# Splitting 64-bit weights on a Trainium2 core: from the square and six mask operations to a scaled copy, a sign and five operations

## The chip, the cores and the metric

The kernel runs on one core of one Trainium2 chip. The metric is the device time of one execution in microseconds. Three executions of the kernel before took 776.67, 776.81 and 775.69 us; the median is 776.67 us.

## What is computed

All inputs are stored as 64-bit floating-point numbers. Three stages follow one another: attention in which a query sees only the keys of its own cluster, a feed-forward layer with a quadratic gate, and a gated layer behind a normalisation.

```python
q_assign = np.argmax(np.einsum('bhsd,hcd->bhsc', q_n, c_n), axis=-1)   # 2 x 8 heads, 768 tokens, 64 wide, 16 clusters
k_assign = np.argmax(np.einsum('bhsd,hcd->bhsc', k_n, c_n), axis=-1)
mask = q_assign[:, :, :, None] == k_assign[:, :, None, :]
attn = softmax(where(mask, scale * q @ k.T, -1e9)) @ v
...
h = x @ w_in                                    # x: 1536 x 512, w_in: 512 x 2048
g = np.where(h >= 1, h, np.where(h <= -1, 0.0, (h + 1) ** 2 / 4))
x = g @ w_out                                   # 2048 x 512
...
xn = x / np.sqrt(np.mean(x * x, axis=-1, keepdims=True) + 1e-06) * rms_g
g, val = xn @ w_gate, xn @ w_val                # 512 x 1536 each
out = (g / (1.0 + np.exp(-g)) * val) @ w_out2   # 1536 x 512
```

## The kernel before

**Products of two halves.** TensorE multiplies numbers that are rounded to a short form. Each factor x is held as a high part, x rounded to that form, and a low part, the rest; a product takes three matmuls, high by high, high by low and low by high. Activations are rounded by ScalarE (a cast) and the rest is taken by VectorE or POOL (a subtraction).

**Weights.** The weights come as 92 slices of 128 x 512 numbers, in the order of the list `stream`. 68 of them are loaded: SP issues two transfers for each (`w_load`, L512), which bring the high 32-bit words (`raw`), and the words one 16-bit step further on (`mid`). `conv_ops` (L546) turns them into the high part `w[:, 0]` and the low part `w[:, 1]`: one square of ScalarE (L565, or L572 while `pace["on"]` is false, in the attention's last part) and six operations of VectorE (L566, L568, L570, L576, L578, L580). The square is large where the number is large enough to matter, and L576 uses it to drop the smallest numbers. L566, L570 and L578 are one-input mask operations; L568 (mask and or), L576 and L580 take two inputs.

**Sums of gate weights.** The other 24 slices are not loaded. They are sums and differences of halves of the gate and value weights, which let the gated layer do with seven products (`term_unit`) in place of eight. `w_sums` (L526) queues six additions for each pair of weights; POOL makes them (L534), one behind each operation of a conversion. A slice of such a sum is converted by one cast of ScalarE (L557) and one subtraction of VectorE (L559). In the order printed below the sums are `s_0` and `s_1`.

**The order of the work.** The program writes all engines' instructions in one order. `units()` is the list of the steps of TensorE (each 0.6 to 2.8 us long by the planner's own numbers); `unit()` issues one and adds its time to `pace["pe"]`. `drain()` issues what the steps before need next on the other engines. Then `fill()` (L1011) issues conversion operations as long as the time that the planner has counted for VectorE, `pace["dve"]`, with the cost of the next one stays below `pace["pe"]`. Each engine works off its own instructions in the order in which they were issued.

**The two places that matter here.** (1) Behind the first layer, `turn_pair` (L728) transposes two tiles of Y and forms three combinations of them: ScalarE copies v (L751) and casts (L752, L753), VectorE subtracts (L756 to L758), ScalarE casts the four results (L762) and POOL takes the rests (L764). It does so four times; ahead of each the tiles Y are completed by an addition of VectorE (L802) and squared by ScalarE for the normalisation (L830). (2) In the gated layer each group of 128 columns is computed by seven terms. Term 1 goes into a bank of accumulators B, term 5 into E, term 2 into A. ScalarE copies B to u before term 6 adds to it, E to e before term 3 does, B to v before term 7 does, and B to w before term 4 does (all L713). TensorE has to wait for each of these copies before it may go on in that bank. ScalarE's silu (L672), the cast of a finished gate (L668) and, for the third block of tokens, the casts of transposed tiles (L863) lie in between.

Of the kernel before, what the change touches and what calls it, by code (L numbers as in the profile page):

```python
# [28 lines left out]
GROUPS2 = [3, 3, 3, 3]  # L29
NPLACES = 24  # L30
LOCK = 0.3
HB = 6
NP = B * H // 2
HALF = S // 2
# [6 lines left out]
def clustered_attention_two_ffn(  # L41
# [464 lines left out]


    W = {}
    stream = []
    cv = {"loaded": 0, "at": 0, "ops": [], "left": 0, "limit": 6, "soon": NPLACES - 6}  # L510

    def w_load():  # L512
        n = cv["loaded"]
        cv["loaded"] += 1
        layer, i, m = stream[n]
        if m < 0:
            return
        rows = slice(128 * m, 128 * m + 128)
        src = (w_in[m], w_out[rows])[i] if layer == 1 else (w_gate[m], w_val[m], w_out2[rows])[i]
        raw, mid, t = fp["raw"](n)  # L520
        nc.sync.dma_start(raw.rearrange("p n w -> p (n w)"), src.bitcast(U32))

        nc.sync.dma_start(mid.rearrange("p n w -> p (n w)").bitcast(U16)[:, 0:2047], src.bitcast(U16)[:, 1:2048])
        cv[n] = (raw[:, :, 1], mid[:, :, 0], t, raw[:, :, 0].bitcast(F32))
# [4 lines left out]
    def w_sums(i, m, w, f):  # L529
# [8 lines left out]
        if i == 0:  # L538
            fp["f"] = f
            return  # L540
        f1, f2 = fp.pop("f"), f
        s, r = (pf.tile([128, 512], F32, tag="s", bufs=3, name=f"s{m}_{n}") for n in range(2))
        op(s[:, left], f2[:, left], f2[:, right], ALU.add)
# [5 lines left out]
    def conv_ops(n):  # L549
# [11 lines left out]
        hi, mid, t, sq = cv.pop(n)  # L561
        tf = t.bitcast(F32)

        if pace["on"]:
            nc.scalar.activation(sq, hi.bitcast(F32), AF.Square, scale=2.0 ** 15)  # L565
        nc.vector.tensor_scalar(t, hi, 3, 0x3FFFF000, op0=ALU.logical_shift_left, op1=ALU.bitwise_and)  # L566
        yield
        nc.vector.scalar_tensor_tensor(t, hi, 0xC0000000, t, op0=ALU.bitwise_and, op1=ALU.bitwise_or)  # L568
        yield
        nc.vector.tensor_scalar(mid, mid, 0x01FFFFFF, None, op0=ALU.bitwise_and)  # L570
        if not pace["on"]:
            cv["square"] = lambda: nc.scalar.activation(sq, hi.bitcast(F32), AF.Square, scale=2.0 ** 15)  # L572
        yield
        square()

        nc.vector.scalar_tensor_tensor(w[:, 0], sq, 1.125 * 1.125, tf, op0=ALU.is_ge, op1=ALU.mult)  # L576
        yield
        nc.vector.tensor_scalar(t, w[:, 0].bitcast(U32), 0xFF800000, None, op0=ALU.bitwise_and)  # L578
        yield
# [5 lines left out]
    def conv(n_ops=1):  # L585

        for _ in range(n_ops):
            if not cv["ops"]:
                if cv["at"] >= cv["limit"] or not room():
                    return False  # L590
                while cv["loaded"] <= cv["at"]:
                    w_load()
                cv["ops"] = [conv_ops(cv["at"])]
                cv["left"] = 6 if stream[cv["at"]][2] >= 0 else 2
                cv["at"] += 1
            pace["dve"] += cost()
            next(cv["ops"][0])
            tick()
            cv["left"] -= 1
            if fp["gp"]:  # L600
                fp["gp"].pop(0)()
            if not cv["left"]:
                cv["ops"] = []
            while cv["loaded"] < cv["limit"] and not any(m >= 0 for _, _, m in stream[cv["at"]:cv["loaded"]]):
                w_load()
# [399 lines left out]
    pace = {"on": False, "pe": 0.0, "dve": 0.0, "post": 0.0}  # L1005

    def cost():
        m, n = (stream[cv["at"] - 1][2], cv["left"]) if cv["ops"] else (stream[cv["at"]][2], 6) if cv["at"] < len(stream) else (0, 0)
        return (0.6 if n == 1 else 0.0) if m < 0 else (0.6 if n % 2 else 0.335) + LOCK * bool(fp["gp"])

    def fill():  # L1011

        while pace["on"] and pace["dve"] + cost() <= pace["pe"] + SLACK[layer_of()]:
            if not conv(1):
                break

# [320 lines left out]
```

## Time and profile before

| | |
|---|---|
| median of three runs | 776.67 us (775.69 to 776.81) |
| the profiled execution | 775.95 us, span 774.2 us |
| TensorE busy | 768.3 us, 99% of the span |
| VectorE busy | 609.9 us, 79% |
| ScalarE busy | 391.9 us, 51% |
| POOL busy | 288.9 us, 37% |
| chain that ended last | PE 92%, DVE 2%, ACT 2%, DMA 1%, POOL 1% |

In the rows, PE is TensorE, DVE VectorE, ACT ScalarE and SP the engine that issues the transfers. A row of a timeline gives the start and the duration of an instruction, and in brackets how long its engine sat idle before it and what ended that. The times of matmuls overlap: what a matmul takes in a row of matmuls is read from one start to the next, not from its duration. The span is the time from the first to the last instruction, and the execution's own time is 1.75 us longer.

### The profile page before, as it was taken

The numbers are of one execution on the slowest core, as the hardware profiler recorded it, in microseconds if no ns is written. First come the engines' busy times: TensorE is split into PE (matmuls) and PEld (weight loads), VectorE is DVE, ScalarE is ACT, GpSimd is POOL, SyncE is SP. The second block draws the span as 40 slices with busy tenths as digits, with TensorE's granted clock in tenths as the row PEclk, the third lists the DMA queues.
The fourth block names the chain that finished last, engine by engine and source line by source line (L and its number), as shares of the span: only waits on it lengthen the run. The fifth ranks groups of instructions, "written<-read, shape, count | busy, mean of one in ns | idle before, by whom it ended". The sixth has DMA issues, their size and how long they took to land.

```text
span 774.2 us, 10868 instructions
## 1 busy us (share of the span) xinstructions
PE 768.3 (99%) x3714; PEld 592.0 (76%) x3714; DVE 609.9 (79%) x1106; ACT 391.9 (51%) x758; POOL 288.9 (37%) x313
## 2 busy tenths in 40 slices
PE   8999999999999999999999999999999999999998
PEld 4666666776558888888888888878888888888887
DVE  6776887776578999877668768899999799988743
ACT  7676767665567655444334447544545315423430
POOL 5878999998000000000001206441454334423400
PEclk9999999999999999999999999999999999999999
DMA  7657665573144676444334310125563343434013
GB/s 202 173 138 182 156 150 131 150 172 113 55 142 143 218 237 218 170 137 163 109 109 136 99 37 0 32 95 181 187 213 109 104 160 128 154 109 163 1 41 123
DMA packets 32679, 103.41 MB, mean 134 GB/s; under 512 B 5016, under 2 KB 5356, under 8 KB 32624
## 3 DMA queue, kind: packets, MB, share of 16 engines
q1 hardware_dynamic: 32612, 102.72, 43.8%
q8 instruction: 29, 0.48, 0.3%
q14 instruction: 26, 0.21, 0.1%
q10 hardware_dynamic: 12, 0.00, 0.0%
HBM read 81.02 MB, written 3.15 MB: 109 GB/s over the span
## 4 chain that ended last, share of the span: by engine, by line
PE 92%; DVE 2%; ACT 2%; DMA 1%; POOL 1%; issue 1%; ACTq 0%; DVEq 0%; POOLq 0%
PE h L624 25%; PE y L788 9%; PE y L787 9%; PE y L786 9%; PE pv L406 8%; PE B L651 8%; PE mp L336 5%; PE sc L385 4%; PE sc L386 4%; PE E L651 4%; PE A L651 2%; PE sum L425 1%; DMA kraw<-kT 1%; PE simt L171 1%; PE sum L414 1%
## 5 line engine op out<-in xcount | busy, mean ns | idle before, releaser
L338 DVE TENSOR_REDUCE M<-mp 128x1 f32<-128x384 f32 x186 | 94.6, 552 | 44.6 <-PE mp L336 44.4
L534 POOL TENSOR_TENSOR bits<-place 128x256 f32<-128x256 f32 x18 | 17.6, 1000 | 265.5 <-DVE place L580 265.5
L398 POOL TENSOR_TENSOR acc<-acc,P 128x384 f32<-128x384 f32 x112 | 109.2, 1004 | 4.1 <-ACT P L388 3.5
L388 ACT ACTIVATE P<-sc 128x384 f32<-128x384 f32 x192 | 82.3, 490 | 42.1 <-PE sc L386 34.1
L624 PE MATMUL h<-xh,aa 128*128 128x512 f32 x280 | 89.3, 390 | 0.1
L802 DVE TENSOR_TENSOR Y<-y,Y 128x512 f32<-128x512 f32 (+1 forms) x85 | 57.8, 681 | 39.6 <-PE y L788 39.3
L639 ACT ACTIVATE a<-h,half_b 128x512 f32<-128x512 f32 x48 | 33.0, 687 | 81.4 <-PE h L624 80.4
L406 PE MATMUL pv<-P,v 128*64 128x384 f32 x384 | 70.6, 492 | 0.0
L385 PE MATMUL sc<-aa,bb 112*128 112x384 f32 x192 | 66.1, 344 | 0.0
L386 PE MATMUL sc<-aa,bb 97*128 97x384 f32 x192 | 65.0, 338 | 0.0
L624 PE MATMUL h<-xh,bb 128*128 128x512 f32 x200 | 64.2, 389 | 0.0
L624 PEld LDWEIGHTS h<-xh,aa 128*128 128x128 f32 x280 | 52.5, 188 | 12.9 <-DVE a L641 0.8
L565 ACT ACTIVATE raw<-raw 128x512 f32<-128x512 f32 x62 | 42.2, 680 | 38.1 <-DMA raw<-w_out 12.4
L641 DVE SCALAR_TENSOR_TENSOR a<-h,a 128x512 f32<-128x512 f32 x48 | 33.1, 690 | 29.7 <-ACT a L640 29.7
L624 PE MATMUL h<-xl,aa 128*128 128x512 f32 x140 | 54.5, 389 | 0.0
L568 DVE SCALAR_TENSOR_TENSOR bits<-raw,bits 128x512 uint32<-128x512 uint32 x68 | 51.7, 760 | 1.6
L336 PE MATMUL mp<-bb,aa 112*128 112x384 f32 x186 | 52.5, 360 | 0.3
L406 PEld LDWEIGHTS pv<-P,v 128*64 128x64 f32 x384 | 25.4, 136 | 31.4 <-issue 30.3
L336 PEld LDWEIGHTS mp<-bb,aa 112*128 112x128 f32 x186 | 32.2, 189 | 15.3 <-issue 5.5
L624 PEld LDWEIGHTS h<-xh,bb 128*128 128x128 f32 x200 | 37.5, 188 | 7.8
L719 POOL TENSOR_TENSOR w<-w,e 128x512 f32<-128x512 f32 x12 | 16.8, 1396 | 60.9 <-ACT w L713 60.9
L624 PE MATMUL h<-xl,bb 128*128 128x512 f32 x100 | 38.9, 389 | 0.0
(307 smaller groups left out, 1987.3 us busy)
## 6 DMA issues: line engine op xcount, KB each, us to landing
raw<-w_out SPq DMA_DIRECT2D x28, 512.0 KB
mid<-w_out SPq DMA_DIRECT2D x28, 511.8 KB
raw<-w_in SPq DMA_DIRECT2D x16, 512.0 KB
mid<-w_in SPq DMA_DIRECT2D x16, 511.8 KB
raw<-w_gate SPq DMA_DIRECT2D x12, 512.0 KB
raw<-w_val SPq DMA_DIRECT2D x12, 512.0 KB
mid<-w_gate SPq DMA_DIRECT2D x12, 511.8 KB
mid<-w_val SPq DMA_DIRECT2D x12, 511.8 KB
```

The lines of the kernel that those rows point to most:

```text
L336: nc.tensor.matmul(mp, A[0:112, h, 0, 128 * qt:128 * qt + 128], Bk[0:112, h, 0, HALF * n:HALF * n + HALF], start=True, stop=True)
L338: nc.vector.tensor_reduce(st["M2", p][:, j, n:n + 1], mp, axis=AX.X, op=ALU.max)
L385: nc.tensor.matmul(sc, Bk[0:112, h, 0, ks], A[0:112, h, 0, qs], start=True, stop=False)
L386: nc.tensor.matmul(sc, Bk[0:97, h, 1, ks], A[0:97, h, 1, qs], start=False, stop=True)
L388: nc.scalar.activation(P, sc, AF.Exp, scale=0.125)
L398: nc.gpsimd.tensor_tensor(acc, acc, P, op=ALU.add)
L406: nc.tensor.matmul(pv[64 * h:64 * h + 64, 0:HALF], st["v", p][:, h, kt], st["P", p, i, h], start=(kt == 0), stop=(kt == NT - 1))
L624: nc.tensor.matmul(h, w[:, wi, fs], x[:, kc, cs], start=(n == 0), stop=(n == 11))
L651: nc.tensor.matmul(h, w[:, wi, fs], x[xi][:, kc], start=start and n == 0, stop=(n == 5), skip_group_check=not start)
L786: nc.tensor.matmul(y[:, c], g[:, 0, fs], w[:, 0, c], start=(m == m0), stop=False)
L787: nc.tensor.matmul(y[:, c], g[:, 0, fs], w[:, 1, c], start=False, stop=False)
L788: nc.tensor.matmul(y[:, c], g[:, 1, fs], w[:, 0, c], start=False, stop=(m == ms[-1]))
```

## The change

The square and the first two operations of VectorE are replaced. ScalarE now makes a copy of the high words, scaled by 2^-112 (new L571), and then the sign of the high words in their own place (new L572). VectorE shifts and masks the scaled copy (new L580), and the high part is that, times the sign (new L582). The scaling drops the smallest numbers by itself. So a slice takes two operations of ScalarE and five of VectorE. The planner's costs follow (`cost()`, five operations). Besides, `fill()` no longer begins a slice while `landed` of that slice is later than `pace["pe"]`: for a loaded slice `landed` is the planner's estimate of the landing (4.2 per load, one behind the other, and 1.0), and for a sum 8.0 behind the time at which its additions were queued. Behind the first inserted lines the numbers of the changed kernel are higher: L557 becomes L563, L559 L565, L713 L719, L764 L770, L802 L808.

```diff
--- before.py
+++ after.py
@@ -29,6 +29,7 @@
 GROUPS2 = [3, 3, 3, 3]
 NPLACES = 24
 LOCK = 0.3
+LOAD, LAND, SUMS = 4.2, 1.0, 8.0
 HB = 6
 NP = B * H // 2
 HALF = S // 2
@@ -506,6 +507,7 @@
 
 
     W = {}
+    landed = {}
     stream = []
     cv = {"loaded": 0, "at": 0, "ops": [], "left": 0, "limit": 6, "soon": NPLACES - 6}
 
@@ -515,6 +517,8 @@
         layer, i, m = stream[n]
         if m < 0:
             return
+        cv["free"] = max(cv.get("free", 0.0), pace["pe"]) + LOAD
+        landed[n] = cv["free"] + LAND
         rows = slice(128 * m, 128 * m + 128)
         src = (w_in[m], w_out[rows])[i] if layer == 1 else (w_gate[m], w_val[m], w_out2[rows])[i]
         raw, mid, t = fp["raw"](n)
@@ -538,6 +542,8 @@
         if i == 0:
             fp["f"] = f
             return
+        for k in range(2):
+            landed[stream.index((2, k, -m - 1))] = pace["pe"] + SUMS
         f1, f2 = fp.pop("f"), f
         s, r = (pf.tile([128, 512], F32, tag="s", bufs=3, name=f"s{m}_{n}") for n in range(2))
         op(s[:, left], f2[:, left], f2[:, right], ALU.add)
@@ -561,19 +567,19 @@
         hi, mid, t, sq = cv.pop(n)
         tf = t.bitcast(F32)
 
+        def sides():
+            nc.scalar.activation(sq, hi.bitcast(F32), AF.Copy, scale=2.0 ** -112)
+            nc.scalar.activation(hi.bitcast(F32), hi.bitcast(F32), AF.Sign)
+
+        cv["square"] = sides
         if pace["on"]:
-            nc.scalar.activation(sq, hi.bitcast(F32), AF.Square, scale=2.0 ** 15)
-        nc.vector.tensor_scalar(t, hi, 3, 0x3FFFF000, op0=ALU.logical_shift_left, op1=ALU.bitwise_and)
-        yield
-        nc.vector.scalar_tensor_tensor(t, hi, 0xC0000000, t, op0=ALU.bitwise_and, op1=ALU.bitwise_or)
-        yield
+            square()
         nc.vector.tensor_scalar(mid, mid, 0x01FFFFFF, None, op0=ALU.bitwise_and)
-        if not pace["on"]:
-            cv["square"] = lambda: nc.scalar.activation(sq, hi.bitcast(F32), AF.Square, scale=2.0 ** 15)
         yield
         square()
-
-        nc.vector.scalar_tensor_tensor(w[:, 0], sq, 1.125 * 1.125, tf, op0=ALU.is_ge, op1=ALU.mult)
+        nc.vector.tensor_scalar(t, sq.bitcast(U32), 3, 0x7FFFF000, op0=ALU.logical_shift_left, op1=ALU.bitwise_and)
+        yield
+        nc.vector.tensor_tensor(w[:, 0], tf, hi.bitcast(F32), op=ALU.mult)
         yield
         nc.vector.tensor_scalar(t, w[:, 0].bitcast(U32), 0xFF800000, None, op0=ALU.bitwise_and)
         yield
@@ -591,7 +597,7 @@
                 while cv["loaded"] <= cv["at"]:
                     w_load()
                 cv["ops"] = [conv_ops(cv["at"])]
-                cv["left"] = 6 if stream[cv["at"]][2] >= 0 else 2
+                cv["left"] = 5 if stream[cv["at"]][2] >= 0 else 2
                 cv["at"] += 1
             pace["dve"] += cost()
             next(cv["ops"][0])
@@ -1005,12 +1011,14 @@
     pace = {"on": False, "pe": 0.0, "dve": 0.0, "post": 0.0}
 
     def cost():
-        m, n = (stream[cv["at"] - 1][2], cv["left"]) if cv["ops"] else (stream[cv["at"]][2], 6) if cv["at"] < len(stream) else (0, 0)
-        return (0.6 if n == 1 else 0.0) if m < 0 else (0.6 if n % 2 else 0.335) + LOCK * bool(fp["gp"])
+        m, n = (stream[cv["at"] - 1][2], cv["left"]) if cv["ops"] else (stream[cv["at"]][2], 5) if cv["at"] < len(stream) else (0, 0)
+        return (0.6 if n == 1 else 0.0) if m < 0 else (0.6 if n in (1, 3) else 0.335) + LOCK * bool(fp["gp"])
 
     def fill():
 
         while pace["on"] and pace["dve"] + cost() <= pace["pe"] + SLACK[layer_of()]:
+            if not cv["ops"] and landed.get(cv["at"], 0.0) > pace["pe"]:
+                break
             if not conv(1):
                 break
```

TensorE's and SP's instructions keep their order. On the other three engines the change moves instructions. The first place is ScalarE at the beginning of the gated layer. In the rows below, u, e, v and w are the copies out of the banks, `s_0` and `s_1` the sums of gate weights that are cast, and a the silu. Before:

```order
L713 COPY u_5190<-B_5183 128x512
L713 COPY e_5211<-E_5204 128x512
L672 ACTIVATE a_0_0_5213<-A_5194 128x512
L713 COPY v_5234<-B_5183 128x512
L713 COPY u_5251<-B_5244 128x512
L672 ACTIVATE a_0_1_5253<-E_5204 128x512
L557 CAST place_3133<-s_0_4740 128x512
L557 CAST bb_110<-s_1_4741 128x512
L713 COPY w_5268<-B_5183 128x512
```

After the change:

```order
L719 COPY u_5193<-B_5186 128x512
L563 CAST aa_105<-s_0_4759 128x512
L563 CAST aa_109<-s_1_4760 128x512
L719 COPY e_5217<-E_5210 128x512
L678 ACTIVATE a_0_0_5219<-A_5200 128x512
L719 COPY v_5240<-B_5186 128x512
L719 COPY u_5257<-B_5250 128x512
L678 ACTIVATE a_0_1_5259<-E_5210 128x512
L571 ACTIVATE raw_5093<-raw_5093 128x512
L572 ACTIVATE raw_5093<-raw_5093 128x512
L719 COPY w_5278<-B_5186 128x512
```

The two casts of sums have moved from behind the second silu to directly behind the first copy u, ahead of the first copy e; and the two operations of a loaded slice now stand ahead of w.

The second place is POOL at the fourth transposed pair (`t_0`, `t_1` are the pair's combinations; `bits` holds sums on the way). Before:

```order
L764 TENSOR_TENSOR xl<-t_0_5120,xh 128x2x128
L764 TENSOR_TENSOR aa_109<-t_0_5120,bb_108 128x2x128
L764 TENSOR_TENSOR bb_110<-t_1_5121,aa_105 128x2x128
L764 TENSOR_TENSOR place_3129<-t_1_5121,aa_107 128x2x128
L534 TENSOR_TENSOR s_0_4740<-bits_4573 128x256
L534 TENSOR_TENSOR s_0_4740<-s_0_4740,bits_4535 128x256
L534 TENSOR_TENSOR s_1_4741<-bits_4535,bits_4573 128x256
L534 TENSOR_TENSOR s_1_4741<-bits_4535,s_0_4740 128x256
```

After the change:

```order
L538 TENSOR_TENSOR s_0_4759<-bits_4642 128x256
L770 TENSOR_TENSOR xl<-t_0_5123,xh 128x2x128
L770 TENSOR_TENSOR place_3128<-t_0_5123,aa_105 128x2x128
L770 TENSOR_TENSOR bb_110<-t_1_5124,aa_107 128x2x128
L770 TENSOR_TENSOR aa_107<-t_1_5124,place_3132 128x2x128
L538 TENSOR_TENSOR s_0_4759<-s_0_4759,bits_4575 128x256
L538 TENSOR_TENSOR s_1_4760<-bits_4575,bits_4642 128x256
L538 TENSOR_TENSOR s_1_4760<-bits_4575,s_0_4759 128x256
```

One of the four additions that make `s_0` and `s_1` now stands ahead of the pair's four subtractions, three still stand behind them.

The third place is VectorE ahead of the same pair. Before:

```order
L802 TENSOR_TENSOR Y<-y_3_11_0_5070,Y 128x512
L566 TENSOR_SCALAR bits_4696<-raw_4694 128x512
L802 TENSOR_TENSOR Y<-y_4_8_0_5097,Y 128x512
L756 TENSOR_TENSOR t_0_5120<-v_5122,xt_5110 128x256
L756 TENSOR_TENSOR t_0_5120<-xt_5115,t_0_5120 128x256
```

After the change:

```order
L808 TENSOR_TENSOR Y<-y_3_11_0_5070,Y 128x512
L577 TENSOR_SCALAR mid_4713<-mid_4713 128x512
L580 TENSOR_SCALAR bits_4714<-raw_4712 128x512
L808 TENSOR_TENSOR Y<-y_4_8_0_5100,Y 128x512
L762 TENSOR_TENSOR t_0_5123<-v_5125,xt_5113 128x256
L762 TENSOR_TENSOR t_0_5123<-xt_5118,t_0_5123 128x256
```

Between the two additions to Y, one operation of a conversion stood before; now two do.

## Rows read from the trace of the kernel before

**Rows 1.** The page, part 1: busy time, share of the span, instructions of each engine.
```profile
PE 768.3 (99%) x3714; PEld 592.0 (76%) x3714; DVE 609.9 (79%) x1106; ACT 391.9 (51%) x758; POOL 288.9 (37%) x313
```

**Rows 2.** The chain of waits, 430 to 450 us: start us, us, piece.
```profile
437.50 8.16 PE h L624 x36
```

**Rows 3.** Timeline of TensorE, 494 to 509 us: start us, us, engine, line, operation.
```profile
495.31 0.39 PE L651 MATMUL E<-xh,aa 128*128 128x512 f32 x1
...
502.60 0.40 PE L651 MATMUL E<-xl,place 128*128 128x512 f32 x1
503.09 0.73 PE L651 MATMUL E<-xh,place 128*128 128x512 f32 x2
...
507.25 0.39 PE L651 MATMUL B<-aa,bb 128*128 128x512 f32 x1
507.73 0.50 PE L651 MATMUL E<-xh,bb 128*128 128x512 f32 x1
508.06 0.39 PE L651 MATMUL E<-xl,bb 128*128 128x512 f32 x1
```

**Rows 4.** Timeline, 576 to 578 us: of ScalarE two rows, then TensorE.
```profile
576.34 0.62 ACT L668 CAST bb<-a 128x512 fp32r<-128x512 f32 x1 [3.78 <-DVE a L676]
576.87 0.58 ACT L713 COPY w<-B 128x512 f32<-128x512 f32 x1
...
577.13 0.39 PE L651 MATMUL B<-xh,aa 128*128 128x512 f32 x1
577.51 0.50 PE L651 MATMUL B<-aa,bb 128*128 128x512 f32 x1
```

**Rows 5.** Groups of instructions, by form: busy us, mean ns, idle before and releaser.
```profile
L568 DVE SCALAR_TENSOR_TENSOR bits<-raw,bits 128x512 uint32<-128x512 uint32 x68 | 51.7, 760 | 1.6
...
L565 ACT ACTIVATE raw<-raw 128x512 f32<-128x512 f32 x62 | 42.2, 680 | 38.1 <-DMA raw<-w_out 12.4 <-DMA raw<-w_in 8.5 <-DMA raw<-w_val 6.4
```

**Rows 6.** Timeline of VectorE, 482 to 491 us.
```profile
483.00 0.97 DVE L566 TENSOR_SCALAR bits<-raw 128x512 uint32<-128x512 uint32 x1
...
490.45 0.42 DVE L570 TENSOR_SCALAR mid<-mid 128x512 uint32<-128x512 uint32 x1
490.78 0.68 DVE L802 TENSOR_TENSOR Y<-y,Y 128x512 f32<-128x512 f32 x1
```

**Rows 7.** Timeline of POOL, 482 to 497 us.
```profile
482.96 0.72 POOL L764 TENSOR_TENSOR place<-t,aa 128x256 fp32r<-128x256 f32 x1
...
493.33 0.73 POOL L764 TENSOR_TENSOR place<-t,aa 128x256 fp32r<-128x256 f32 x1
494.02 0.91 POOL L534 TENSOR_TENSOR s<-bits 128x256 f32<-128x256 f32 x1
495.02 0.75 POOL L534 TENSOR_TENSOR s<-s,bits 128x256 f32<-128x256 f32 x1
495.72 0.73 POOL L534 TENSOR_TENSOR s<-bits,bits 128x256 f32<-128x256 f32 x1
496.42 0.73 POOL L534 TENSOR_TENSOR s<-bits,s 128x256 f32<-128x256 f32 x1
```

**Rows 8.** Timeline of ScalarE, 492 to 503 us.
```profile
492.52 0.57 ACT L713 COPY u<-B 128x512 f32<-128x512 f32 x1
494.21 0.59 ACT L713 COPY e<-E 128x512 f32<-128x512 f32 x1 [1.12 <-PE E L651]
...
501.60 0.61 ACT L557 CAST place<-s 128x512 fp32r<-128x512 f32 x1
502.11 0.62 ACT L557 CAST bb<-s 128x512 fp32r<-128x512 f32 x1
```

**Rows 9.** Timeline of ScalarE, 211 to 214 us, in the attention's last part.
```profile
211.53 0.69 ACT L572 ACTIVATE raw<-raw 128x512 f32<-128x512 f32 x1
212.29 0.48 ACT L419 COPY pvs<-pv 128x384 f32<-128x384 f32 x1
213.48 0.87 ACT L388 ACTIVATE P<-sc 128x384 f32<-128x384 f32 x2 [0.71 <-PE sc L386]
```

## The prediction, made before the changed kernel was run

> **What bounds the kernel now.** I read the page's busy shares first [rows 1]: TensorE is busy 99% of the span, VectorE 79% and ScalarE 51%. Hence an instruction taken off VectorE or put on ScalarE is worth nothing by itself; it counts only where TensorE waits for it. Second, the chain of waits: in the second half of the program it is long pieces of TensorE alone, and its piece of 36 matmuls in 8.16 us [rows 2] gives the pitch of a 512-column matmul, 8.16 / 36 = 0.227 us. Third, I held TensorE's rows of the feed-forward half against that pitch and looked for starts that come late. There are few, and all the larger ones stand where the gate terms hand sums between engines: 502.60 to 503.09 is 0.49 us for one matmul, 507.25 to 507.73 is 0.48, 507.73 to 508.06 is 0.33 [rows 3], and 577.13 to 577.51 is 0.38 [rows 4]. So the extra time is 0.26, 0.25, 0.10 and 0.15 us. The third of these is no wait of its own: the first matmul after a stall costs about 0.10 us more than the pitch. I add that restart to each stall. With it these stalls cost about 1.0 us in all (0.26 + 0.25 + 0.15 and three restarts), so a change that makes VectorE or ScalarE faster has little to win, and one that makes either late at one of these places can lose more.
>
> **What is removed and added.** For each of the 68 converted slices VectorE loses one operation: before six, of which the combined mask-and-or takes 760 ns [rows 5]; now five. That is 68 x 0.76 = 51.7 us. ScalarE gets one more: two of about 0.68 us [rows 5] for one, 68 x 0.68 = 46.2 us. The second of these, the sign, is not in the trace; its bounds are the copy, 0.57 [rows 8], and the scaled square, 0.68 [rows 5], and I take the upper. TensorE waits for neither of the two on most slices, because a slice is converted well before its first matmul. In the attention's last part ScalarE makes the softmax that TensorE waits for, so there an extra operation could hurt. It lies between pieces of other work: after the square at 211.53 ScalarE still has 0.71 us idle before the exponentials at 213.48 [rows 9]. An extra 0.68 in front of them fits, barely. I take 0 for this part; without that cover each of the 68 - 62 = 6 slices converted in this form there would cost up to 0.68 us.
>
> The wait that the gate adds is in the program's planner, not on the chip: it only decides at which unit a slice's first operation is issued. It moves conversions later when the load was issued a short time before; the instructions held back by it are those of conversion alone. ScalarE's waits for weights are 12.4 us for the rows from the output weights [rows 5], and TensorE felt none of them, so I take 0 for this too, with bounds of 0 and of one such wait if a slice is converted too late; in the planner's order no conversion is forced at its use.
>
> **Where the order moves against TensorE.** The place is the transposed-pair stage at 480 to 510 us. The first sums of gate weights, s_0 and s_1, are made by POOL and rounded by ScalarE's casts. Before, these two casts stand behind the copies u, e, v, u, and run at 501.60 and 502.11 [rows 8]. Now they stand right behind the first u copy and **ahead of the first e copy**, because conversion runs further ahead of its old place and the gate counts its 8 us from the time the sums were queued, which is long past. ScalarE goes in order, so e now waits for POOL to finish s_1. POOL's four subtractions of the fourth pair end at 493.33 + 0.73 = 494.06, and its adds run 494.02, 495.02, 495.72 and 496.42 [rows 7]. Now one of the four adds stands ahead of the subtractions, and three behind them.
>
> What TensorE then waits for, step by step. (1) VectorE has one conversion operation more ahead of the sum Y that releases the chain Y, square, v copy, pair differences, casts, POOL: two for one. Such an operation took 0.33 us from start to start at 490.45, but 0.97 at 483.00 [rows 6], beside a POOL subtraction at 482.96 [rows 7]; two at 0.33 in place of one at 0.97 would be a gain of 0.31, one more at 0.97 a loss of 0.97. I take +0.33, the nearer row, since it lies in the very pair and the other ran beside POOL's work that now stands elsewhere. (2) So POOL's adds begin at 494.02 + 0.33 = 494.35, and three of them end 0.70 + 0.70 + 0.73 later [rows 7], at 496.48. (3) The second cast starts then and the e copy 0.51 us behind it (the pitch of the two casts, [rows 8]), at 496.99; e takes 0.59 and ends at 497.6. (4) TensorE needs e for the matmul that started at 495.31 [rows 3]. It starts 2.3 us late, plus the restart of 0.10: **+2.4 us**. By the bounds of step 1 it is +1.8 to +3.0 (2.4 - 0.64 and 2.4 + 0.64).
>
> The Trainium skill, page "SBUF — State Buffer", section "SBUF: two separate sides", says that a VectorE operation in a two-port mode, or one with two inputs in SBUF, and a POOL operation hold a shared port pair for the whole instruction, so that the later one blocks. By that rule the extra operation costs the longer of the two times of step 1 when POOL is busy, and this step would give the upper end of +3.0. The operation of 0.97 us beside POOL's subtraction agrees with it; the one of 0.42 at 490.45 [rows 6] is no test of it.
>
> **What is given back.** The stall at 502.60 was a wait for the low half of the slice whose cast stood at 501.60; with the cast some 6 us earlier it is gone: -0.26, and of the two matmuls from 503.09 (0.57 us for two, [rows 3]) -0.11. At 577.13 TensorE waits for the w copy of 576.87, which is queued behind a cast that VectorE released at 576.34 [rows 4]; VectorE with an operation less per slice comes earlier there: -0.15 - 0.10. The wait at 507.25 I leave, since ScalarE has more to do there, not less. Together -0.6.
>
> **Sum.** +2.4 - 0.6 = +1.8 us, with ends of 1.8 - 0.6 = +1.2 and of 3.0 (nothing given back). The profiled execution took 775.95 us and would take 777.75; it stood 0.72 below the median of 776.67, so against the median I forecast 776.67 + 1.8 = 778.5, and 777.9 to 779.7 for this case alone.
>
> **Rivals.**
> A, **the block does not reach TensorE**. If POOL's sums were complete before about 493.6 (e waits for its own matmuls until 494.21, [rows 8], and two casts of 0.51 must fit ahead of it; 0.5 us more is free until 495.31), the new order would cost nothing. Then only what is given back counts: 776.67 - 0.6 = 776.1, not slower. For it: the first add has moved ahead of the pair, and POOL is idle for much of the time before the pair. Against it: three adds stand behind the pair's subtractions in POOL's order, and these end at 494.06 already. It decides if the subtractions come 2.5 us earlier than now.
> B, **ScalarE's pairs delay the w copies too**. In several gate groups the two new operations stand directly ahead of w, whose result TensorE takes up at once (577.45 to 577.51 in [rows 4]). Two operations at the pitch of 0.51 us [rows 8] put w up to 1.0 us later, less the slack. Three such places at 0.6 to 1.0 us add 1.8 to 3.0 to the forecast: 780.3 to 781.5. Against it: ScalarE is half idle, and w waits for its matmuls anyway.
> C, **the relief of VectorE reaches TensorE**. The Trainium skill, page "Perfetto Trace Analysis", section "Optimizing Scalar/DVE Operations", says that offloading from VectorE to ScalarE may make sense when VectorE is saturated. VectorE is 79% busy [rows 1], and TensorE's stalls listed above come to 1.0 us; if all of it goes and the block does not come, the time is 775.7. Faster by over 0.2% it is only if 0.6 us more goes, in the attention's part for example, that I don't see in the rows. A variant without any effect, in which the gate holds back nothing and the moved casts are hidden, gives 776.7 and belongs to A.
>
> **How the numbers follow.** A measurement of this kernel can tell about 0.2%, 1.55 us: faster is below 775.1, slower above 778.2. My forecast has a chance of 0.60; as its own range begins at 777.9, I put 0.50 of it above 778.2 and 0.10 below. A has 0.24, all the same. B has 0.08, slower. C has 0.08, and I give it to faster. That makes faster 0.08, same 0.34, slower 0.58. The range reaches below A by the 0.6 us that a given-back term may be off, and takes in the nearer end of B: 775.5 to 780.5. It leaves out the rest of B and of C.
>
> **What would show it.** In the changed kernel's ScalarE rows near 494 us: the two casts ahead of e, with an idle time that ends on POOL's s, and the matmul of E that now starts near 497.7 with a gap of 2 us or more before it. In VectorE's groups: five operations a slice and about 50 us less; in ScalarE's about 46 us more; neither matched in the span. POOL's third add behind the pair should end near 496.5. TensorE's row at 503 and the one at 577 should run at the pitch. It is wrong if e starts by 494.7 (then A), if several w copies end late with gaps in TensorE behind them (B), or if the attention's last part is longer by some 0.7 us a slice.

## The result and the profile after

The changed kernel takes 780.48 us (median of four runs, 779.56 to 780.74) against 776.32 us for the kernel before on the same chip: the ratio is 1.0055, 95% interval 1.0042 to 1.0068. It is slower, as forecast, by 4.2 us where 1.8 were forecast. The profiled execution took 780.57 us, with a span of 778.8 us. Of two of the kernels below one or two executions took over 1200 us; these are left out of their numbers.

Part 1 of the page of the changed kernel, to be held against [rows 1]:

```profile
PE 769.5 (99%) x3714; PEld 592.7 (76%) x3714; DVE 559.4 (72%) x1038; ACT 436.6 (56%) x826; POOL 283.2 (36%) x313
```

VectorE is busy 50.5 us less and ScalarE 44.7 us more, as worked out; TensorE is 99% busy as before. The groups of ScalarE's two operations on a slice (busy us, mean ns, idle before and releaser), to be held against [rows 5]:

```profile
L572 ACT ACTIVATE raw<-raw 128x512 f32<-128x512 f32 x68 | 46.6, 686 | 2.2
L571 ACT ACTIVATE raw<-raw 128x512 f32<-128x512 f32 x68 | 45.9, 675 | 18.7 <-DMA raw<-w_gate 12.2 <-DMA raw<-w_out 5.7 <-DMA raw<-w_in 0.8
```

The sign takes 686 ns, where the upper bound of 0.68 us was taken. What TensorE waited for in the gated half, from its table of waits (us in total, times, longest); in the kernel before no row of that table has 0.3 us or more in this half:

```profile
PE E L657 <- ACT e L719: 2.5, 1, 2.5
...
PE y L794 <- DVE place L671: 0.5, 1, 0.5
...
PE B L657 <- ACT w L719: 0.3, 1, 0.3
```

**The block at the e copy came as forecast.** ScalarE's timeline around the first copies of the gated layer:

```profile
494.81 0.56 ACT L719 COPY u<-B 128x512 f32<-128x512 f32 x1
497.07 0.62 ACT L563 CAST aa<-s 128x512 fp32r<-128x512 f32 x1 [1.70 <-POOL s L538]
498.43 0.62 ACT L563 CAST aa<-s 128x512 fp32r<-128x512 f32 x1 [0.74 <-POOL s L538]
498.96 0.58 ACT L719 COPY e<-E 128x512 f32<-128x512 f32 x1
```

The copy u is done at 495.4, then ScalarE sits idle for POOL twice, casts the two sums, and only then copies e. Before, e started at 494.21 [rows 8]. TensorE's timeline shows the price, a wait of 2.49 us before the first matmul of E behind that copy:

```profile
496.71 0.39 PE L657 MATMUL B<-aa,aa 128*128 128x512 f32 x1
499.59 0.50 PE L657 MATMUL E<-xh,aa 128*128 128x512 f32 x1 [2.49 <-ACT e L719]
```

To find where the rest went I compared the start of each matmul with that of the same matmul before. The difference stands at 1.4 us when the attention ends. It grows by 0.2 just ahead of the wait for the e copy and by 2.8 at it. Then it falls by 1.4 in five steps, because small stalls that the kernel before had at 502 to 508 and at 577 us are gone, and grows by 0.2 at 513 us, where a small stall is new. It grows by 0.7 at 611 and by 0.6 at 666 us. The figures of the three waits hold the restart of about 0.1 us that follows each.

The attention's 1.4 us are no part of the change. In three profiles of the unaltered kernel before, the third matmul behind the attention started at 231.06, 231.59 and 234.09 us, in two of the changed one at 232.46 and 231.47. What follows it repeats far better: from that matmul to TensorE's last one the kernel before took 539.69, 539.70 and 539.70 us in those three, and the changed one 542.91 and 543.01. **In the profiled executions the change costs 3.2 to 3.3 us**, and the interval of the ratio (3.3 to 5.3 us) only just reaches down to it. The rest of the 4.2 is not split up by any run: the attention scatters by more than that, and in six of ten executions of the changed kernel TensorE's mean granted clock was 0.997 or 0.998, while it was 0.999 or 1.000 in the two that were profiled and in every execution of the kernel before whose clock is on record; the last section comes back to this. I use the stretch behind the attention below, under the name of the second half, because it tells kernels apart where medians of whole runs can't.

### The profile page after: what moved, and what is told of

Read it like the earlier page. It is cut to its first block, busy times and chain, and to the rows that moved or that the text cites. A ratio compares the mean times of both kernels' runs of the same rounds, so it can differ in the third digit from the quotient of the medians.

```text
span 778.8 us, 10888 instructions
## 1 busy us (share of the span) xinstructions
PE 769.5 (99%) x3714; PEld 592.7 (76%) x3714; DVE 559.4 (72%) x1038; ACT 436.6 (56%) x826; POOL 283.2 (36%) x313
## 4 chain that ended last, share of the span: by engine, by line
PE 88%; DVE 4%; ACT 3%; POOL 2%; DMA 1%; issue 1%; ACTq 0%; DVEq 0%; POOLq 0%
PE h L630 25%; PE y L794 9%; PE y L793 9%; PE y L792 9%; PE pv L407 8%; PE B L657 7%; PE mp L337 5%; PE sc L386 4%; PE sc L387 4%; PE E L657 3%; PE A L657 1%; PE sum L426 1%; DMA kraw<-kT 1%; PE simt L172 1%; PE sum L415 1%
## 5 line engine op out<-in xcount | busy, mean ns | idle before, releaser
L538 POOL TENSOR_TENSOR bits<-bb 128x256 f32<-128x256 f32 x18 | 15.3, 865 | 290.0 <-issue 234.7
L630 PE MATMUL h<-xh,aa 128*128 128x512 f32 x264 | 84.9, 390 | 0.1
L808 DVE TENSOR_TENSOR Y<-y,Y 128x512 f32<-128x512 f32 (+1 forms) x85 | 57.6, 680 | 32.8 <-PE y L794 32.2
L645 ACT ACTIVATE a<-h,half_b 128x512 f32<-128x512 f32 x48 | 33.0, 687 | 71.3 <-PE h L630 70.8
L630 PE MATMUL h<-xh,bb 128*128 128x512 f32 x192 | 61.7, 389 | 0.0
L630 PEld LDWEIGHTS h<-xh,aa 128*128 128x128 f32 x264 | 49.5, 188 | 12.3 <-issue 1.2
L571 ACT ACTIVATE raw<-raw 128x512 f32<-128x512 f32 x68 | 45.9, 675 | 18.7 <-DMA raw<-w_gate 12.2
L630 PE MATMUL h<-xl,aa 128*128 128x512 f32 x132 | 51.4, 389 | 0.0
L580 DVE TENSOR_SCALAR bits<-raw 128x512 uint32<-128x512 uint32 x68 | 32.9, 485 | 21.7 <-ACT raw L571 21.1
L572 ACT ACTIVATE raw<-raw 128x512 f32<-128x512 f32 x68 | 46.6, 686 | 2.2
L630 PE MATMUL h<-xh,place 128*128 128x512 f32 x120 | 38.7, 389 | 0.0
```

Source lines behind the costliest of these rows:

```text
L630: nc.tensor.matmul(h, w[:, wi, fs], x[:, kc, cs], start=(n == 0), stop=(n == 11))
```

## The experiments

**The changed kernel again.** No edit.

> The changed kernel once more, unaltered. Open is what made its attention part end 1.4 us later in the profile (0.63 us within the first 7 us, 0.25 at 79 us, 0.53 at 104 us), though no conversion runs there. Theory scatter: the shift at 190 us against the kernel before differs by more than 0.5 us in this second profile, and the gated half shows the same three stalls (about 2.7 us at E's first matmul behind the e copy, 0.6 us each at 611 and 666 us). Rival, a fixed cost of the change: the shift is 1.4 us again within 0.2, at the same places. Time 780.4 +- 0.6 by both.

Measured: ratio 1.0051, interval 1.0033 to 1.0069, 780.38 us. The attention ended 0.99 us earlier than in the first profile, the three stalls stood where they had stood, and the second half took 543.01 us against 542.91. So the attention's shift is scatter, and the stalls are fixed.

**The kernel before again, twice.** No edit.

> The kernel before once more, unaltered, for the attention's part alone. In the profiles of the changed family TensorE reaches the end of the attention 0.0 to 1.5 us later than in the one profile of the kernel before. Theory scatter: this second profile of the kernel before ends its attention at least 0.3 us later than the first. Rival (the change costs about 0.7 us there): it ends within 0.2 us of the first. In the gated half the same small stalls stand at 502, 507 and 577 us by both.

> A third profile of the kernel before, with the same two expectations as the second: at least 0.3 us later at the attention's end by scatter, within 0.2 us by a cost of the change.

Measured: 776.49 and 779.00 us, one run each. The attention ended 0.53 and 3.03 us later than in the first profile, the second half took the same to 0.01 us. Scatter again, and it reaches further than the effect under study.

**The casts behind v.**

```diff
-            landed[stream.index((2, k, -m - 1))] = pace["pe"] + SUMS
+            landed[stream.index((2, k, -m - 1))] = 276.5 if m == 1 else pace["pe"] + SUMS
```

> One number differs from the changed kernel: the two casts of sums are held until behind the v copy, three places further on in ScalarE's order; nothing else moves but their subtraction on VectorE. Theory (the casts ahead of e make TensorE wait for POOL): the gap of 2.7 us at the first matmul of E behind the e copy is gone, and the kernel takes 2.0 to 2.9 us less than the changed one, 777.6 to 778.4 (some of the small stalls at 503 to 508 us may come back). Rival (POOL's late sums cost the same wherever they are awaited): a wait of 2 us or more turns up at the next place, the second u copy, and the time stays within 0.5 us of the changed kernel's.

Measured: 778.00 us, ratio 1.0019 (1.0010 to 1.0029), and the gap at the e copy is gone. TensorE's waits in the second half are now these:

```profile
PE xt L865 <- DVE Y L858: 0.8, 2, 0.6
...
PE y L794 <- DVE place L671: 0.5, 1, 0.5
PE B L657 <- ACT w L719: 0.4, 1, 0.4
```

The second half takes 541.75 us, 1.2 less than before the move. The block was worth 2.8; the rest is given back at once, since VectorE's normalised Y, which the block had covered, is now waited for at 500 and at 505 us (0.8 and 0.4 us with what goes with them), and the small stall at 507 us is back. Only the two casts and one subtraction of VectorE behind them have moved, so the order of the casts is shown to be the cause of the block. In the profiled executions the removed wait paid less than half of what it measured. By the medians of the same round it paid 2.4 us (780.38 to 778.00), inside the expectation; with the wait the executions of a granted clock below 0.999 went too (none of eleven, where the changed kernel had four of six in that round).

**Without the sign.** The high parts come out without their sign's factor.

```diff
-            nc.scalar.activation(hi.bitcast(F32), hi.bitcast(F32), AF.Sign)
```

> The changed kernel without the second operation of ScalarE, the sign; the high parts come out without it, so the output is not the reference's. Every other instruction keeps its place. Theory (the second operation delays VectorE and the w copy in line): the stalls at 611 and 666 us, 0.63 and 0.49 us and a restart of 0.1 each, shrink below 0.2 each; the 2.7 us gap at the e copy stays within 0.2; time 1.0 to 1.5 us below the changed kernel, about 779.2. Rival (the stalls come from the order on VectorE and the port shared with POOL): both stay within 0.2 and the time within 0.4.

Measured: 779.78 us, ratio 1.0041 (1.0026 to 1.0055). The wait at 666 us is gone, the one at 611 falls from 0.47 to 0.23 us, the block stays. So the second operation of ScalarE is what makes w late at 666 us, and it is a good part of the stall at 611. The time fell by 0.6 us only, though, less than expected. In its profile TensorE ran slow behind the same block and lost 1.6 us, see the last section; without them its second half of 543.26 us would be 1.3 below the changed kernel's. For the medians this explains little, as the granted clock was 0.998 in six of its seven executions and 0.998 or less in four of six of the changed kernel's; which of the two figures is the sign's worth stays open.

**Without the gate.**

```diff
-            if not cv["ops"] and landed.get(cv["at"], 0.0) > pace["pe"]:
-                break
```

> The changed kernel without the two lines in fill() that hold a slice until its estimated landing. Theory (the cheaper conversion by itself puts the casts ahead of e): the casts stand ahead of e and the gap of 2.5 us or more is still there; the time is within 1.0 us of the changed kernel's. Rival (the gate is what costs): the gap at the e copy is below 1 us, or the time is over 1.5 us lower, near 778. Conversions that begin before their weights have landed should show as longer idle times of ScalarE on transfers, without TensorE waiting.

Measured: 790.6 us, ratio 1.0182 (1.0164 to 1.0201). The block is there, so it is not the gate that puts the casts ahead of e; but the gate matters too. Without it TensorE waits 8.5 us at 300 us. ScalarE's timeline there:

```profile
300.81 0.68 ACT L571 ACTIVATE raw<-raw 128x512 f32<-128x512 f32 x1 [2.05 <-DVE bits L584]
...
304.81 0.68 ACT L571 ACTIVATE raw<-raw 128x512 f32<-128x512 f32 x1 [2.63 <-DMA raw<-w_in]
...
306.08 0.67 ACT L645 ACTIVATE a<-h,half_b 128x512 f32<-128x512 f32 x1
...
308.56 0.60 ACT L674 CAST aa<-a 128x512 fp32r<-128x512 f32 x1
```

ScalarE works in line: it waits for a conversion of VectorE, then 2.63 us for a transfer that has not landed, and only then comes to the gate of the first layer (L645, L646) and its cast (L674) at 308.56, for which TensorE had waited since 300.7. I expected such waits to stay on ScalarE; that was wrong.

**The gate alone**, put into the kernel before, conversions as they were.

```diff
     while pace["on"] and pace["dve"] + cost() <= pace["pe"] + SLACK[layer_of()]:
+        if not cv["ops"] and landed.get(cv["at"], 0.0) > pace["pe"]:
+            break
         if not conv(1):
```

> The kernel before with the gate alone: six operations and the square as they were, but a slice is not begun before its estimated landing. Theory (the gate costs and gives nothing while conversion is slow enough to come behind the landings): within 0.8 us of the kernel before; the casts of sums stay behind the second silu, no wait of TensorE of 1 us or more in the gated half. Rival (the gate shifts work against TensorE by itself): slower by 1.5 us or more with a new gap.

Measured: 794.38 us, ratio 1.0241 (1.0228 to 1.0254), so the rival held, at twelve times its least figure. TensorE waits, at six of its steps, for sums that are cast and subtracted too late. The longest of its waits on them (us in total, times, longest):

```profile
PE E L657 <- ACT place L563: 2.3, 2, 1.4
PE E L657 <- DVE aa L565: 2.3, 1, 2.3
```

The two for `aa` and `place` that are not shown are as long as these. All come to 10.9 us, less than the 18.4 that the kernel loses: the granted clock fell to a mean of 0.61 in one of the stretches behind them (602 to 610 us), and matmuls came every 0.43 us there in place of 0.227.

**The changed kernel, paced as six operations.**

```diff
-        ... (0.6 if n in (1, 3) else 0.335) + LOCK * bool(fp["gp"])
+        ... (0.6 if n in (1, 3) else 0.935 if n == 5 else 0.335) + LOCK * bool(fp["gp"])
```

> The changed kernel with one number of the planner's costs altered: a slice's first operation is counted 0.6 us dearer, so that a slice counts as much as six operations did. Theory (the cheaper cost puts conversion ahead, and with it the casts ahead of e): the casts stand behind the second silu again, the 2.7 us gap is gone, and the time is 2.5 to 4 us below the changed kernel's, within 0.8 of the kernel before. Rival (the form itself, two operations of ScalarE a slice, is what costs): the gap is gone but gaps of 0.5 us and more stand at other gate groups, 778.5 or more.

Measured: 821.49 us, ratio 1.0589 (1.0572 to 1.0606), the worst of all. The first of the casts does stand behind the second silu, the 2.7 us gap is gone, and gaps stand elsewhere, as the rival said. Its reason is not shown: the waits are of the kind that the gate alone brought, with one operation of ScalarE a slice, and longer:

```profile
PE E L657 <- ACT bb L563: 9.6, 3, 3.8
PE E L657 <- DVE bb L565: 7.1, 3, 4.2
```

Both results have one explanation, which the planner's order supports. While a slice is held at the gate, the time that the planner grants VectorE passes unused. A planner that counts 2.8 us a slice then falls behind: in the order that it writes, 27 conversion operations are issued only when TensorE's own step asks for them in the first of these kernels, and 54 in the second; in the kernel before it was one, in the changed kernel none. So the gate, the cheaper conversion and the lower count belong together. Leaving out the gate costs 10 us by the medians (11.6 in the second half), adding it alone costs 18, and raising the count costs 41. The share of the granted clock in these is not worked out; the means over the profiled executions are 0.994, 0.994 and 0.979.

**No slice begun at term 7.** On top of the casts behind v.

```diff
+        pace["hold"] = k == 7
         drain()
+        pace["hold"] = False
...
-            if not cv["ops"] and landed.get(cv["at"], 0.0) > pace["pe"]:
+            if not cv["ops"] and (pace.get("hold") or landed.get(cv["at"], 0.0) > pace["pe"]):
```

> The kernel with the casts behind v, and besides no slice is begun in the step of term 7, so that no scaled copy and sign are issued between that term's matmuls and the copy w. Theory (the pair of operations ahead of w delays it): the stall of 0.5 to 0.6 us at 666 us is below 0.2, the one at 611 us is left or smaller; the time is 0.4 to 1.2 us below that of the kernel with the casts behind v. Rival (the cast that waits for VectorE delays w, not the pair): the stall stays within 0.2 and the time within 0.3.

Measured: 776.56 us, ratio 1.0010 (1.0001 to 1.0018); second half 540.42 us, 1.3 less than with the casts behind v alone. The stalls at 611 and 666 us are both gone. A wait of 1.0 us for the copy e at 509 us has come, behind a scaled copy and a sign.

**The pair before its use.** On top of the casts behind v.

```diff
-        if pace["on"]:
-            square()
         nc.vector.tensor_scalar(mid, mid, 0x01FFFFFF, None, op0=ALU.bitwise_and)
```

> The kernel with the casts behind v, and the scaled copy and the sign are issued only with the second operation of VectorE, the one that reads the copy, as in the attention's part. Theory: VectorE now waits for ScalarE in line at most slices, its waits on the scaled copy and the sign rise from about 24 us to over 40 us; TensorE feels it at one or more sums in the gated half, 0 to 2 us slower than with the casts behind v alone. Rival (the w copies gain more than VectorE loses): the stalls at 611 and 666 us go and it is 0.8 us or more faster.

Measured: 777.77 us, ratio 1.0025 (1.0015 to 1.0036); second half 541.10 us. VectorE's waits on the two operations rise only to 29 us. The stall at 666 us is gone, the one at 611 stays. Neither theory fits whole; it bears out that the pair ahead of w costs, and that VectorE has room to wait.

**No slice begun at terms 5 and 7.** The edit of term 7 with `k in (5, 7)`.

> The kernel with the casts behind v and no slice begun in the steps of term 5 nor of term 7, so that no scaled copy and sign stand directly ahead of a copy e or w. Theory (those pairs in ScalarE's line are what is left): the wait of 1.0 us for the e copy at 509 us, seen with term 7 alone, goes; the wait of 0.6 us for VectorE's normalised Y at 501 us stays; 0.6 to 1.2 us below the kernel that holds at term 7 alone, which was 0.6 us above the kernel before, so 0 to 0.6 us below the kernel before. Rival (the work held back falls on other copies): a wait of 0.5 us or more at another e, u or w, and the time within 0.3 of the one that holds at term 7.

Measured: 776.4 us, ratio 1.0005 (0.9996 to 1.0014); second half 540.14 us, 0.3 below the kernel that holds at term 7 alone where 0.6 to 1.2 were expected. The wait at 509 us is gone and the one for Y at 501 us stays, as expected, but two matmuls at 510 us that start 0.3 and 0.5 us late take much of the gain. VectorE's timeline ahead of the wait at 501 us shows the small operations of the normalisation, 4 columns each, while POOL adds up the last sums:

```profile
496.38 0.66 DVE L847 SCALAR_TENSOR_TENSOR rt<-rr 128x4 f32<-128x4 f32 x1
497.07 0.66 DVE L848 TENSOR_TENSOR rt<-rt,ssq 128x4 f32<-128x4 f32 x1
497.77 0.67 DVE L849 SCALAR_TENSOR_TENSOR rr<-rt,rr 128x4 f32<-128x4 f32 x1
```

**The sums ahead of the pair.** The same, and

```diff
-            if fp["gp"]:
-                fp["gp"].pop(0)()
+            for _ in range(3):
+                if fp["gp"]:
+                    fp["gp"].pop(0)()
```

> As the kernel with no slice begun at terms 5 and 7, and besides up to three of POOL's queued additions are issued behind each operation of a conversion in place of one, so that the four additions of s_0 and s_1 all stand ahead of the fourth pair's subtractions. Theory (VectorE's small normalising operations took 0.67 us in place of 0.16 because POOL was adding beside them): most of them take 0.16 to 0.2, the wait of 0.6 us for the normalised Y at 501 us goes, and the kernel is 0.3 to 0.9 us below the one without this and faster than the kernel before. Rival (additions in longer runs block VectorE's conversion and sums elsewhere through the shared port): the wait at 501 us goes but others of 0.3 us and more appear, and the time stays within 0.3 or rises.

Measured: 775.59 us, ratio 0.9993 (0.9984 to 1.0002); second half 539.51 us. The same operations of VectorE with POOL's additions out of the way:

```profile
496.87 0.16 DVE L848 SCALAR_TENSOR_TENSOR rt<-rr 128x4 f32<-128x4 f32 x1
497.07 0.16 DVE L849 TENSOR_TENSOR rt<-rt,ssq 128x4 f32<-128x4 f32 x1
497.26 0.16 DVE L850 SCALAR_TENSOR_TENSOR rr<-rt,rr 128x4 f32<-128x4 f32 x1
```

The wait at 501 us is gone; waits of 0.5 us for u at 495 us and 0.3 for w at 647 us are new, so both the theory and a part of its rival came. This version undoes the whole cost of the change. That it beats the kernel before isn't shown: its second half is 0.2 us shorter, and the interval holds 1.

## Why the prediction was right in kind and short in size

**The number.** Forecast were 778.5 us, 1.8 above the kernel before; measured were 780.48, 4.2 above, of which the second half of the profiles shows 3.2. The range of the forecast itself ended at 779.7. That 780.48 lies inside the wide range, 0.02 us below its end of 780.5, is luck: that end was set by the near end of rival B.

**Which place and which wait: right.** The casts ahead of e, the wait on POOL's last addition, the restart behind it and the direction all came as the prediction put them, and moving nothing but those casts and their subtraction took the gap away.

**Its size: 2.4 forecast, 2.8 measured, and step 1 is why.** I took +0.33 us for the conversion operation that was added ahead of Y, from the row at 490.45, and said that it "lies in the very pair". That was a misreading. The row stands between later additions to Y, behind the differences of the fourth pair; the one operation between the two additions to Y ahead of the fourth pair is the row at 483.00 [rows 6], and the addition behind it started 0.89 us later:

```profile
483.89 0.68 DVE L802 TENSOR_TENSOR Y<-y,Y 128x512 f32<-128x512 f32 x1
```

VectorE's timeline of the changed kernel at that place:

```profile
484.40 0.98 DVE L577 TENSOR_SCALAR mid<-mid 128x512 uint32<-128x512 uint32 x1
485.30 0.97 DVE L580 TENSOR_SCALAR bits<-raw 128x512 uint32<-128x512 uint32 x1
486.19 0.68 DVE L808 TENSOR_TENSOR Y<-y,Y 128x512 f32<-128x512 f32 x1
```

The two operations take 1.79 us up to the addition, where the one took 0.89. That is +0.90, almost the upper bound. POOL's timelines show what ran beside them and what followed, first before, behind the subtraction at 482.96 [rows 7]:

```profile
483.65 0.94 POOL L534 TENSOR_TENSOR bits<-bb 128x256 f32<-128x256 f32 x1
```

and after the change:

```profile
484.36 0.73 POOL L770 TENSOR_TENSOR aa<-t,place 128x256 fp32r<-128x256 f32 x1
485.05 0.94 POOL L538 TENSOR_TENSOR bits<-bb 128x256 f32<-128x256 f32 x1
486.06 0.80 POOL L538 TENSOR_TENSOR s<-bits 128x256 f32<-128x256 f32 x1
492.82 0.94 POOL L770 TENSOR_TENSOR xl<-t,xh 128x256 fp32r<-128x256 f32 x1 [5.96 <-ACT xh L768]
...
495.61 0.73 POOL L770 TENSOR_TENSOR aa<-t,place 128x256 fp32r<-128x256 f32 x1
496.30 0.73 POOL L538 TENSOR_TENSOR s<-s,bits 128x256 f32<-128x256 f32 x1
497.00 0.72 POOL L538 TENSOR_TENSOR s<-bits,bits 128x256 f32<-128x256 f32 x1
497.68 0.72 POOL L538 TENSOR_TENSOR s<-bits,s 128x256 f32<-128x256 f32 x1
```

POOL's subtraction at 484.36 and its addition at 485.05 ran beside the two operations, as the same two had run beside the one before. In the trace of the kernel before, the same kind of operation (L566, L570, L578) took 0.41 to 0.43 us in all 164 cases without a POOL operation beside it, and 0.42 to 1.53 us, 0.82 in the mean, in the 40 beside one. The Trainium skill, page "SBUF — State Buffer", section "SBUF: two separate sides", states such a block for operations that need the shared port pair, and the rows at this place agree with it: by that rule the prediction had +3.0, nearer than my choice. My reason, that POOL's work "now stands elsewhere", was an error too: these two instructions of POOL had not moved, and the addition that did move, at 486.06, starts only 0.2 us before the second operation ends. Steps 2 to 4 held: the three additions end 2.06 us behind the subtractions where 2.13 were taken, the second cast starts 0.03 us later, and e 0.53 behind it. With +0.90 in step 1 the sum of the prediction gives +3.0, which is what came: the late pair delays the copy u too, so that 0.2 us of it show just ahead and 2.8 at e.

**What is given back: 0.6 forecast, 1.2 measured.** The two places that I had counted came as counted: 0.36 us at 503 (forecast 0.26 and 0.11) and 0.26 at 577 us (0.15 and 0.10). The stall at 507 us, which I had left in, went too (0.35), and so did two small ones at 502 and 504 us that I had not listed (0.27 and 0.17); 0.23 us at 513 us are new.

**Added operations beside TensorE's work: costed at 0, and this step failed.** The sentence was that TensorE waits for neither of the two on most slices, and the sum had no term for those where it does. It cost 1.3 us at two places of the second half. At 666 us it is rival B:

```profile
664.02 0.62 ACT L674 CAST aa<-a 128x512 fp32r<-128x512 f32 x1 [2.71 <-DVE a L682]
664.54 0.67 ACT L571 ACTIVATE raw<-raw 128x512 f32<-128x512 f32 x1
665.25 0.67 ACT L572 ACTIVATE raw<-raw 128x512 f32<-128x512 f32 x1
665.82 0.57 ACT L719 COPY w<-B 128x512 f32<-128x512 f32 x1
```

The last of TensorE's matmuls ahead of w had started at 664.37. ScalarE came to w only behind a cast and the two operations of a slice, and TensorE waited 0.33 us and lost 0.6 with the restart. At 611 us a sum waits for the low half of a gate:

```profile
610.10 0.57 DVE L584 TENSOR_SCALAR bits<-bb 128x512 uint32<-128x512 uint32 x1
610.60 1.22 DVE L671 TENSOR_TENSOR place<-a,place 128x512 fp32r<-128x512 f32 x1
```

The subtraction at 610.60 takes 1.22 us in place of 0.69, beside a POOL addition, and stands behind a conversion operation of 0.57. That the sign is a part of this stall is shown by the kernel without it; how much is the order of VectorE's and POOL's instructions is not. I had looked at where ScalarE's load lies as a sum over slices and checked the attention's last part place by place, but not the twelve w copies; a reader of the order could have counted which of them had the pair directly ahead. They are four (at 506, 540, 580 and 665 us), and only the last made TensorE wait. Rival B had three such places at 0.6 to 1.0 us and only 0.08 of the chance; one place at 0.6 came, and it was no rival to the block but came on top of it. That is the mistake in how the cases were set up: cases that do not exclude one another were given as if they did.

**The attention's last part: 0, right.** From 190 us to the end of the attention no profile of the changed kernel took longer than the kernel before. **The gate at 0: right as a sum, wrong as a reason.** The changed kernel as a whole has no forced conversion and no wait for a landing on TensorE's path; but the gate is worth 10 to 12 us to it. I weighed only what the gate adds, not what the cheaper conversion does without it.

Together: +2.8 at e, +0.2 just ahead of it, -1.2 given back, +0.7 at 611 and +0.6 at 666 us with restarts, +3.1 us of the 3.2 to 3.3 of the second half; the rest is spread over matmuls in steps of under 0.05 us. The other 0.9 of the measured 4.2 is not split up: the attention's scatter and the slow stretches of the last section can both be in it.

## What to carry to other kernels

On engines that work in line, an operation taken off or put on is worth what it does to the order: look at each copy that the bound engine waits for, and at what now stands directly ahead of it and what that waits for in turn. Price an operation of VectorE by whether POOL runs beside it at that place in the new order (here 0.42 us alone, 0.82 in the mean beside one), and add up mechanisms that can occur together before chances are given to any. A planner's cost, its gate and the work itself form one setting; taken alone each of the parts tried here was worse than either whole.

## What the runs showed of the hardware that was not expected

**The clock behind a wait.** In the kernel without the sign TensorE waited 2.53 us at the e copy, and the stretches around it (us, busy by engine, granted clock in the third column from the end) were:

```profile
490.00:496.00 6.00, 6.00 (x27) 4.78 (x26) 4.96 (x10) 3.65 (x11) 3.11 (x4) 1.00 0.35 111
499.00:502.00 3.00, 2.32 (x6) 1.85 (x7) 2.66 (x12) 1.60 (x4) 1.33 (x2) 0.69 0.00 0
502.00:505.00 3.00, 3.00 (x11) 2.39 (x10) 2.96 (x6) 0.62 (x2) 0.00 (x0) 0.75 0.00 0
```

In the changed kernel, behind a wait of 2.49 us at the same place, they were:

```profile
490.00:496.00 6.00, 6.00 (x27) 4.72 (x26) 4.96 (x10) 3.65 (x11) 3.18 (x4) 1.00 0.33 114
499.00:502.00 3.00, 2.41 (x10) 1.99 (x11) 2.66 (x11) 1.51 (x4) 1.25 (x2) 1.00 0.00 0
502.00:505.00 3.00, 3.00 (x17) 2.49 (x16) 2.96 (x6) 0.79 (x2) 0.00 (x0) 1.00 0.01 3
```

With the granted clock at a mean of 0.69 and 0.75, between the levels of 1.2 and 2.4 GHz, matmuls came every 0.43 us for some eight of them, in place of 0.227, which is 1.6 us in all. So waits of the same length may or may not be followed by a slow stretch. The mean granted clock of the whole execution without the sign was 0.998. Of ten executions of the changed kernel six had 0.998 or 0.997, and none of the eleven with the casts behind v, where the wait is gone, had less than 0.999. So the wait at e seems to bring a slow stretch in most executions, though not in the two that were profiled, and it then costs more than they show; which executions had one, no profile tells. Behind the wait of 8.5 us without the gate the clock had fallen while TensorE sat idle, and stood at the lower level, a mean of 0.50, for longer:

```profile
290.00:299.00 9.00, 9.00 (x42) 7.44 (x41) 7.37 (x15) 6.58 (x12) 0.00 (x0) 1.00 0.72 237
300.00:309.00 9.00, 0.67 (x3) 0.21 (x2) 5.89 (x12) 5.44 (x9) 0.00 (x0) 0.77 0.82 279
309.00:313.00 4.00, 3.24 (x7) 2.13 (x8) 3.97 (x9) 3.31 (x7) 0.00 (x0) 0.50 0.56 173
```

**Small operations pay the whole block.** A VectorE operation on 4 columns takes 0.16 us alone and 0.65 to 0.67 beside POOL's additions, see the two timelines above. Beside them its time follows POOL's instruction, not its own size: in the first of the two, POOL's additions ended at 497.02 and 497.72 us, VectorE's operations at 497.04 and 497.73.
